# Two layers of linear attention and gated MLP on one core: GpSimd in the plan as exclusive with VectorE, GpSimd takes some rows, key weight first, new leads

## The chip, the cores and the metric

The kernel runs on 1 core of one Trainium2 chip. A core has five engines, each with its own instruction stream: TensorE (PE in the profile, with PEld for its weight loads), VectorE (DVE), ScalarE (ACT), GpSimd (POOL) and SyncE (SP, which only issues transfers here). The metric is device time in microseconds (us) for one execution. The kernel before takes 412.57 us, the median of 3 runs (409.76 to 413.67).

## The reference

The input is x, 2048 rows of 512 in bf16. Two layers, with the same weights in both, each do `x = x + A(layernorm(x))` and `x = x + B(layernorm(x))`:

```
def A(x):                                   # 32 heads of 16
    q, k, v = split(x @ wqkv)
    pq, pk = q @ w_phi, k @ w_phi           # per head, 16 x 16
    phi_q = concat(softmax(pq), softmax(-pq))
    phi_k = concat(softmax(pk), softmax(-pk))
    kv, z = phi_k.T @ v, phi_k.sum(rows)    # over all 2048 rows
    return ((phi_q @ kv) / (phi_q @ z + 1e-6)) @ wo
def B(x):                                   # F = 1376
    gate, up = x @ W_gate, x @ W_up
    return (relu(gate) * up) @ W_down
```

The sums kv and z run over all rows, so in each layer no row's attention can end before every row's keys are done.

## The kernel before

**Tiling.** The 16 tiles of 128 rows are worked in five slabs of 2, 4, 4, 4 and 2 tiles. All of x stays in SBUF (`x_sb`), as do the weights. For a slab, the names of stages are a letter code, the layer and the slab: `la` (layernorm before attention), `k` (keys and values), `q` (queries), `z` and `at` (denominators), `sp` (spreading the denominators over the features and scaling), `nm` (numerators), `wo` (output projection), `lg` (layernorm before the MLP), `gl` (gate and up), `d` (down projection); `fk` and `fq` fold w_phi into the key and query weights once.

**Layernorm** (`layernorm`, L720 on): VectorE takes statistics (L730, L731), ScalarE takes logarithm and exponential for the inverse deviation (L733, L735), and the row is normalized ("apply") on ScalarE (L747, for which VectorE first makes `nmr`, L739) or on VectorE (L750). TensorE then transposes the tile: four tiles at a time in 32 by 32 tiles of its array (L775), or one tile by four whole transposes (L612); ScalarE or VectorE copies the result into `yT` (L690, L693).

**Keys** (`keys`, L786 on): per tile, keys and values are multiplied (L799, L801, whose instructions carry the helper's line L608), two exponentials run on ScalarE (L803), VectorE sums them per head (`Zk`, L805) and takes the reciprocal (`rZk`, L807), the value is copied to `vsb`, and two products `vhat` of `vsb` and `rZk` (both in SBUF, 544 elements per partition) run on GpSimd, or on VectorE where a table says so (L815). TensorE adds exp(k) times vhat up in 128 x 32 tiles (L827) and VectorE adds the slab's sum to `kvsum` (L843). `sums` (L845) then spreads it into the block matrices `ZD` and `kvbd`.

**Attention** (`attend`, L874 on): `zz` and `zd` on TensorE, `Zs` on ScalarE, `zm`, `zden` on VectorE, logarithm and exponential on ScalarE (`zr`), `aT` on VectorE (L902). For slabs 0 and 1 a matmul spreads aT over the features (L973) and VectorE scales the exponentials `expq` by it (L988, L991). For slabs 2 to 4 aT goes out to DRAM and comes back spread (L912, L916), and `scale` multiplies four parts of expq by `abT` on VectorE (L958). Then the numerators (L928), their copies `oT`, and the output projection.

**Start.** TensorE runs eight warm-up matmuls. The key weight `Wknat` is transposed with w_phi's block matrix `BD` folded in: 16 transposes, four copies (`ftk0` to `ftk3`), 16 small matmuls, four casts into `Wkp` (`fck0` to `fck3`). SP issues x tile 0, x tile 1, the value weight wv, x tiles 2 to 7 and so on; ScalarE's queue issues w_phi and then the key weight in two halves.

**What sets the order.** Nothing is ordered by hand. `Program.op` collects operations with a planned occupancy and latency each. `schedule` lists them in order of a simulated clock: at each step it takes, over all engines, the ready operation with the smallest (start minus bonus, priority), and priority is the operation's number minus its stage's entry in the table `LEAD`; `BONUS` is a table too. `ENG` says per piece of work which engine does it. `plan` then puts semaphore waits where data depends on another engine. So the clock only fixes each engine's order; on the chip an engine runs its list and waits for semaphores.

An operation may be marked `port=True`. The plan then starts it no earlier than the end of the last GpSimd operation, and keeps GpSimd free until it ends:

```
if o.port and ported > s:
    s = ported
...
if o.port:
    free["pool"] = max(free["pool"], s + o.occ)
if o.eng == "pool" and not o.is_dma:
    ported = s + o.lat
```

Before, the mark stands at the apply on VectorE (L750) and at the scalings of expq with both inputs in SBUF (L958, L988). No semaphore comes of it.

Of the kernel before, what the change touches and what calls it, by code (L numbers as in the profile page):

```python
# [20 lines left out]
LEAD = {'': 1581,  # L21
 'at00': -9,
 'at01': -1074,
 'at02': -507,
 'at03': -757,
 'at10': -335,
 'at11': 762,
 'at12': -656,
 'at13': 331,
 'at14': -567,  # L30
 'd00': -5820,
 'd01': -1699,
 'd02': -13878,
 'd03': -2622,
 'd04': 3155,
 'd10': -13359,
 'd11': -2460,
 'd12': -1931,
 'd13': 71,
 'd14': -310,  # L40
 'fk': -480,
 'gl00': -2522,
 'gl01': 1205,
 'gl02': -5857,
 'gl03': -1218,
 'gl04': 504,
 'gl10': -2926,
 'gl11': -481,
 'gl12': -7344,
 'gl13': -46,  # L50
 'gl14': -166,
 'k00': 4572,
 'k01': 869,
 'k02': 459,
 'k03': -281,
 'k04': -136,
 'k10': 388,
 'k11': -124,
 'k12': -1352,
 'k13': 414,  # L60
 'k14': -1,
 'la00': -523,
 'la01': -375,
 'la02': 9240,
 'la03': 2125,
 'la04': -103,
 'la10': -743,
 'la11': -3565,
 'la12': -1372,
 'la14': 7230,  # L70
 'lg00': 199,
 'lg01': -221,
 'lg02': 153,
 'lg04': -687,
 'lg11': -282,
 'lg12': -264,
 'lg13': 794,
 'lg14': 2775,
 'nm00': 842,
 'nm01': 32,  # L80
 'nm02': 3263,
 'nm03': -579,
 'nm04': 406,
 'nm10': -741,
 'nm12': 16,
 'nm13': -1558,
 'nm14': -3291,
 'q00': 5078,
 'q01': -515,
 'q02': -692,  # L90
 'q03': 3551,
 'q04': -1249,
 'q10': -241,
 'q11': -69,
 'q12': -281,
 'q13': -2355,
 'q14': -138,
 'sp00': 803,
 'sp01': 206,
 'sp02': 643,  # L100
 'sp03': 36,
 'sp04': 2026,
 'sp10': 11,
 'sp11': -275,
 'sp12': -193,
 'sp13': -604,
 'sp14': 1242,
 'su0': -202,
 'su1': -6,
 'wo00': -564,  # L110
 'wo01': -1486,
 'wo02': -805,
 'wo03': -998,
 'wo04': 84,
 'wo10': 477,
 'wo11': 1154,
 'wo12': -216,
 'wo13': -222,
 'wo14': -8,
 'z00': -275,  # L120
 'z01': -232,
 'z02': -28,
 'z03': -803,
 'z04': 287,
 'z10': -247,
 'z11': 1911,
 'z12': 85,
 'z13': -5,
 'z14': 170}
BONUS = {'': 400,  # L130
 'at00': 1500,
 'at01': 400,
 'at02': 200,
 'at03': 200,
 'at04': 200,
 'at10': 400,
 'd03': 200,
 'd11': 800,
 'd12': 200,
 'fk': 400,  # L140
 'fq': 200,
 'gl03': 200,
 'gl04': 200,
 'gl11': 200,
 'gl12': 1500,
 'k12': 200,
 'la00': 400,
 'la01': 200,
 'la13': 200,
 'lg10': 400,  # L150
 'nm00': 200,
 'nm04': 200,
 'q11': 200,
 'sp00': 200,
 'sp01': 200,
 'sp03': 200,
 'sp10': 400,
 'sp11': 200,
 'sp13': 200,
 'su0': 800,  # L160
 'su1': 1500,
 'wo04': 400,
 'wo10': 400,
 'wo13': 200,
 'wo14': 200,
 'z03': 200,
 'z04': 200,
 'z10': 200,
 'z12': 400,
 'z13': 200}  # L170
HOLD = {}
ENG = {'ap/a00/0': 'act',
 'ap/a01/0': 'dve',
 'ap/a01/1': 'dve',
 'ap/a01/3': 'dve',
 'ap/a02/0': 'dve',
 'ap/a02/3': 'dve',
 'ap/a03/0': 'dve',
 'ap/a10/1': 'act',
 'ap/a11/1': 'act',  # L180
 'ap/a12/1': 'act',
 'ap/a12/2': 'act',
 'ap/a13/0': 'act',
 'ap/a13/3': 'act',
 'ap/a14/1': 'act',
 'ap/g01/0': 'act',
 'ap/g01/1': 'act',
 'ap/g01/3': 'act',
 'ap/g02/0': 'act',
 'ap/g02/3': 'act',  # L190
 'ap/g11/0': 'act',
 'ap/g12/2': 'act',
 'ap/g13/0': 'act',
 'ap/g13/2': 'act',
 'ap/g13/3': 'act',
 'ap/g14/1': 'act',
 'em/01/00': 'act',
 'em/01/01': 'dve',
 'em/01/02': 'act',
 'em/11/02': 'act',  # L200
 'em/11/03': 'dve',
 'fck3': 'act',
 'ftk0': 'dve',
 'ftq2': 'dve',
 'ftq3': 'dve',
# [3 lines left out]
 'ot/01/2': 'dve',  # L209
 'ot/01/3': 'dve',  # L210
 'ot/02/1': 'dve',
 'ot/02/2': 'dve',
 'ot/02/3': 'dve',
 'ot/03/3': 'dve',
 'ot/04/1': 'dve',
 'ot/04/2': 'dve',
 'ot/04/3': 'dve',
 'ot/10/2': 'dve',
 'ot/11/1': 'dve',
 'ot/13/0': 'dve',  # L220
 'ot/14/0': 'dve',
 'ot/14/1': 'dve',
 'ot/14/2': 'dve',
 'vc/0/5': 'dve',
 'vc/0/6': 'dve',
 'vc/1/0': 'dve',
 'vc/1/12': 'dve',
# [4 lines left out]
 'vc/1/8': 'dve',  # L232
 'vc/1/9': 'dve',
 'vh/0/10/1': 'dve',
 'vh/0/13/1': 'dve',
 'vh/0/15/0': 'dve',
 'vh/0/15/1': 'dve',
 'vh/0/7/0': 'dve',
 'vh/0/9/0': 'dve',
 'vh/1/0/1': 'dve',  # L240
 'vh/1/1/0': 'dve',
 'vh/1/10/0': 'dve',
 'vh/1/14/1': 'dve',
 'vh/1/15/0': 'dve',
 'vh/1/15/1': 'dve',
 'vh/1/3/1': 'dve',
 'vh/1/4/1': 'dve',
 'vh/1/5/0': 'dve',
 'vh/1/8/1': 'dve',
 'yc/a01/01': 'act',  # L250
 'yc/a01/03': 'act',
 'yc/a02/00': 'act',
 'yc/a02/03': 'act',
 'yc/a03/00': 'act',
 'yc/a03/02': 'act',
# [3 lines left out]
 'yc/a10/02': 'dve',  # L259
 'yc/a11/03': 'act',  # L260
 'yc/a12/01': 'act',
 'yc/a12/03': 'act',
 'yc/a13/00': 'dve',
 'yc/g00/1': 'dve',
 'yc/g01/00': 'dve',
 'yc/g01/01': 'act',
 'yc/g01/03': 'act',
 'yc/g02/00': 'dve',
 'yc/g04/00': 'dve',
 'yc/g04/02': 'dve',  # L270
 'yc/g04/03': 'act',
 'yc/g10/0': 'dve',
 'yc/g10/1': 'dve',
 'yc/g11/02': 'dve',
 'yc/g11/03': 'act',
 'yc/g12/01': 'act',
 'yc/g13/02': 'dve',
 'yc/g14/02': 'dve',
 'yc/g14/03': 'act'}
# [29 lines left out]
class Op:  # L309
    __slots__ = ("idx", "eng", "fn", "reads", "writes", "occ", "lat", "name", "is_dma", "nbytes",  # L310
                 "deps", "odeps", "users", "missing", "ready", "start", "finish", "cnt", "stream", "prio", "bonus", "port")

    def __init__(self, idx, eng, fn, reads, writes, occ, lat, name, is_dma=False, nbytes=0):
        self.idx, self.eng, self.fn = idx, eng, fn
        self.reads, self.writes = list(reads), list(writes)
        self.occ, self.lat, self.name = float(occ), float(lat), name
        self.is_dma, self.nbytes = is_dma, nbytes
        self.deps, self.odeps, self.users = set(), set(), []
        self.missing, self.ready = 0, 0.0
        self.start = self.finish = self.cnt = self.stream = None  # L320
        self.prio = idx
        self.bonus, self.port = 0.0, False


class Program:
# [4 lines left out]
    DMA_BW = 270.0  # L330

# [4 lines left out]
    def op(self, eng, fn, reads=(), writes=(), occ=100.0, lat=None, name="", bonus=0.0, port=False):  # L336
        o = Op(len(self.ops), eng, fn, reads, writes, occ, occ + 100.0 if lat is None else lat, name)
        o.bonus, o.port = bonus + BONUS.get(self.tag, 0.0), port
# [54 lines left out]
    def schedule(self):  # L393
        self.derive()
        free = {e: 0.0 for e in ENGINES}
        qfree = ported = 0.0
        ready = {e: [] for e in ENGINES}
# [9 lines left out]
        while left:  # L407
# [25 lines left out]
            for b in new_banks(o):  # L433
# [4 lines left out]
                if old is not None:  # L438
                    for x in old.ops:
                        if x.eng != "pe":  # L440
                            o.deps.add(x.idx)
            o.start = s
            if o.port:
# [83 lines left out]
def build_kernel(nc, A_x, A_wqkv, A_w_phi, A_wo, W_gate, W_up, W_down, out):  # L527
# [8 lines left out]
    with ExitStack() as ctx:  # L536
# [96 lines left out]

        load_x(0, 1)
        load_x(1, 2)
        dma("act", lambda e: e.dma_start(wphi[:], A_w_phi.rearrange("(kc hl) d f -> (hl d) kc f", hl=8)),
            writes=[R("wphi")], nbytes=131072, name="ld wphi")
        for c in (0, 2):
            dma("act", (lambda c: lambda e: e.dma_start(Wknat[:, c:c + 2, :], wqkv_v[:, c:c + 2, 512:1024]))(c),
                writes=R_Wnat["k"][c:c + 2], nbytes=262144, name="ld wk")  # L640
# [18 lines left out]
        op("dve", lambda e: e.memset(ones, 1.0), writes=[R("ones")] + [R("yT", NYT - 1, i) for i in range(4)], occ=480, name="ones")  # L659
# [5 lines left out]
        for i in range(NWARM):  # L665
            op("pe", lambda e: e.matmul(full(warm), ones[:, 0:128], ones[:, 0:512], start=True, stop=True),
               reads=[R("ones"), R("yT", NYT - 1, 0)], writes=[warm], occ=427, lat=640, name="warm")
        op("pool", lambda e: e.affine_select(ident[:], ones[:, 0:128], [[1, 128]], ALU.is_equal, 0.0, base=0, channel_multiplier=-1),
           reads=[R("ones"), R("yT", NYT - 1, 0)], writes=[R("ident")], occ=260, name="ident")
        op("pool", lambda e: e.affine_select(mask8a[:], ones[:, 0:8], [[-16, 8]], ALU.is_ge, 0.0, base=0, channel_multiplier=1),  # L670
           reads=[R("ones"), R("yT", NYT - 1, 0)], writes=[R("mask8a")], occ=150, name="mask8a")
# [48 lines left out]
        def layernorm(key, st, steps):  # L720
# [4 lines left out]
            for gi, step in enumerate(steps):  # L725
# [12 lines left out]
                if "act" in engs:  # L738
                    op("dve", (lambda t0, step: lambda e: e.scalar_tensor_tensor(nmr[:, t0:t0 + step, :], mv[:, t0:t0 + step, 0:1], -1.0, rstd[:, t0:t0 + step, :], ALU.mult, ALU.mult))(t0, step),  # L739
                       reads=Rmv + Ry, writes=[R("nmr", t) for t in ts], occ=75, lat=165, name="nmr")  # L740
                ybs = []
                for t, eng in zip(ts, engs):
# [6 lines left out]
                    else:  # L749
                        op("dve", (lambda t, yb: lambda e: e.tensor_scalar(ytile[:, yb, :], x_sb[:, t, :], mv[:, t, 0:1], rstd[:, t, :], op0=ALU.subtract, op1=ALU.mult))(t, yb),  # L750
# [385 lines left out]
```

## Time and profile before

| | |
|---|---|
| time, median of 3 runs | 412.57 us (409.76 to 413.67) |
| profiled execution | 414.23 us |
| its span, first to last instruction | 412.5 us |
| mean granted TensorE clock | 0.992 |
| TensorE busy | 396.0 us, 96% of the span |
| VectorE, ScalarE, GpSimd busy | 293.2, 209.5, 56.2 us |

An engine is busy while it has an instruction in flight; matmuls are pipelined, so their durations overlap, and "busy" is the union. A row of the timeline gives the start from the span's beginning, the length, the engine, the line of the kernel, the operation, what it writes and reads, its shape and the number of merged instructions; in brackets, how long the engine was idle before and who ended that. Instructions of helpers carry the helper's line: L608 is every plain matmul, L612 every whole transpose, L690 and L693 every copy on VectorE and ScalarE.

### The profile page before, as it was taken

The page shows a single profiled execution, that of the slowest core. Times are in us where ns is not written, and L with a number is a line of the kernel's source. Part 1 is how long each engine was busy: PE and PEld are TensorE (multiplying, and loading weights), DVE is VectorE, ACT ScalarE, POOL GpSimd, SP SyncE. Part 2 cuts the span into 40 slices and gives each one's busy share as a digit, 9 for nine tenths or more (in the row PEclk, how much of TensorE's full clock was granted, in tenths as well). Part 3 has the DMA queues.
Part 4 walks back from the last instruction along what each step waited for, and adds up shares of the span by engine and source line. Part 5 has one row for each costly group of instructions (what it writes and reads, how often), then busy time and mean ns, then how long its engine had stood idle before and what let it go on. Part 6 is the DMA issues. An engine that isn't in the chain of part 4 may idle for free.

```text
span 412.5 us, 11244 instructions
## 1 busy us (share of the span) xinstructions
PE 396.0 (96%) x4879; PEld 208.4 (51%) x4879; DVE 293.2 (71%) x586; ACT 209.5 (51%) x434; POOL 56.2 (14%) x55
## 2 busy tenths in 40 slices
PE   6899997999999998999999999999999999999997
PEld 3544543564444444445445745557444444444475
DVE  4899998897367779793988489638996354762253
ACT  4998998455304772247421477987335213432220
POOL 0068670000000232000600027000000000000000
PEclk9999998999999999999999999999999999999999
DMA  8960000300000003000100000011320000010011
GB/s 269 338 217 3 3 2 5 108 4 0 2 0 2 2 5 107 2 2 5 52 2 2 2 2 3 9 53 56 112 66 13 27 27 1 13 40 2 0 35 43
DMA packets 17922, 16.83 MB, mean 41 GB/s; under 512 B 3056, under 2 KB 16848, under 8 KB 17872
## 3 DMA queue, kind: packets, MB, share of 16 engines
q1 hardware_dynamic: 16656, 15.50, 11.6%
q8 instruction: 38, 0.62, 0.6%
q10 hardware_dynamic: 1216, 0.61, 0.5%
q14 instruction: 12, 0.10, 0.1%
HBM read 13.68 MB, written 2.42 MB: 39 GB/s over the span
## 4 chain that ended last, share of the span: by engine, by line
PE 79%; DVE 13%; ACT 3%; DMA 2%; issue 1%; POOL 1%; ACTq 0%; DVEq 0%
PE pb L608 72%; DVE Zk L805 3%; PE pb L886 2%; DVE vhat L815 2%; PE pb L775 2%; PE pb L827 2%; DMA hT<-in_A_wqkv_dram 1%; DVE stats L730 1%; DVE rZk L807 1%; PE pb L928 1%; DMA abT<-spread 1%; ACT expk L803 1%; PE pb L612 1%; DVE expq L991 1%; DVE vsb L690 1%
## 5 line engine op out<-in xcount | busy, mean ns | idle before, releaser
L1018 ACT ACTIVATE gate_sb<-pb 128x512 bf16<-128x512 f32 (+2 forms) x90 | 52.8, 587 | 113.0 <-PE pb L608 112.9
L1020 DVE TENSOR_TENSOR hT<-gate_sb,pb 128x512 bf16<-128x512 bf16 (+2 forms) x90 | 59.7, 670 | 64.5 <-PE pb L608 62.9
L608 PE MATMUL pb<-yT,Wu 128*128 128x512 bf16 (+3 forms) x440 | 94.6, 337 | 0.0
L608 PE MATMUL pb<-yT,Wg 128*128 128x512 bf16 (+3 forms) x440 | 92.6, 337 | 0.0
L815 POOL TENSOR_TENSOR vhat<-vsb,rZk 128x544 bf16<-128x544 bf16 x48 | 55.3, 1177 | 197.8 <-DVE rZk L807 116.6
L608 PE MATMUL pb<-Wd,hT 128*128 128x512 bf16 (+2 forms) x363 | 81.2, 373 | 0.0
L608 PEld LDWEIGHTS pb<-yT,Wg 128*128 128x128 bf16 (+1 forms) x440 | 43.2, 100 | 32.9 <-issue 0.7
L608 PEld LDWEIGHTS pb<-yT,Wu 128*128 128x128 bf16 (+1 forms) x440 | 43.1, 100 | 31.8 <-issue 0.6
L995 DVE TENSOR_TENSOR x_sb<-x_sb,pb 128x512 bf16<-128x512 bf16 x59 | 39.2, 680 | 22.8 <-PE pb L608 22.6
L608 PEld LDWEIGHTS pb<-Wd,hT 128*128 128x128 bf16 (+1 forms) x363 | 34.8, 98 | 39.4 <-issue 0.8
L803 ACT ACTIVATE expk<-pb 128x512 bf16<-128x512 f32 x64 | 35.4, 621 | 10.2 <-PE pb L608 8.8
L730 DVE BATCH_NORM_STATS2 stats<-x_sb 128x6 f32<-128x512 bf16 x60 | 39.4, 675 | 0.9 <-DMA x_sb<-in_A_x_dram 0.5
L805 DVE TENSOR_REDUCE Zk<-expk 128x64 f32<-128x1024 bf16 x32 | 37.6, 1189 | 1.7 <-ACT expk L803 1.6
L871 ACT ACTIVATE expq<-pb 128x512 bf16<-128x512 f32 x64 | 33.5, 623 | 6.1 <-PE pb L608 6.1
L608 PE MATMUL pb<-wv,yT 128*128 128x512 bf16 x128 | 34.5, 382 | 0.3 <-ACT expk L803 0.3
L608 PE MATMUL pb<-Wkp,yT 128*128 128x512 bf16 x128 | 34.1, 380 | 0.0
L608 PE MATMUL pb<-wo_sb,oT 128*128 128x512 bf16 x128 | 31.7, 392 | 0.8 <-ACT oT L693 0.8
L608 PE MATMUL pb<-yT,Wqp 128*128 128x512 bf16 (+1 forms) x160 | 31.6, 337 | 0.4 <-DVE yT L690 0.3
L693 ACT ACTIVATE yT<-pb 128x512 bf16<-128x512 bf16 (+1 forms) x36 | 19.5, 593 | 15.4 <-PE pb L775 14.4
L733 ACT ACTIVATE lnv<-mv,eps 128x4 f32<-128x4 f32 (+2 forms) x25 | 7.7, 307 | 34.7 <-DVE mv L731 34.2
L747 ACT ACTIVATE ytile<-x_sb,nmr,rstd 128x512 bf16<-128x512 bf16 x27 | 20.9, 815 | 1.4 <-DVE nmr L739 1.3
L608 PEld LDWEIGHTS pb<-wo_sb,oT 128*128 128x128 bf16 x128 | 12.2, 100 | 16.0 <-DVE oT L690 1.7
(77 smaller groups left out, 328.9 us busy)
## 6 DMA issues: line engine op xcount, KB each, us to landing
abT<-spread SPq DMA_DIRECT2D x32, 128.0 KB
out_dram<-x_sb SPq DMA_DIRECT2D x15, 128.0 KB, 4.0
x_sb<-in_A_x_dram SPq DMA_DIRECT2D x3, 512.0 KB
Wg<-in_B_W_gate_dram SPq DMA_DIRECT2D x1, 1376.0 KB
Wu<-in_B_W_up_dram SPq DMA_DIRECT2D x1, 1376.0 KB
Wd<-in_B_W_down_dram SPq DMA_DIRECT2D x1, 1280.0 KB
abT<-spread SPq DMA_DIRECT2D x16, 64.0 KB
hT<-in_A_wqkv_dram ACTq DMA_DIRECT2D x2, 256.0 KB
```

Source lines behind the costliest of these rows:

```text
L608: op("pe", lambda e: e.matmul(view(ps), lhsT, rhs, start=start, stop=stop), reads=reads, writes=[ps], occ=max(25.0, 0.4167 * n + 2.6), lat ...
L693: op("act", lambda e: e.activation(dst(), src(), ACT.Copy), reads=[ps] + reads, writes=writes, occ=115 + 0.714 * n, lat=240 + 0.714 * n, n ...
L730: op("dve", (lambda t, src: lambda e: e.bn_stats(stats[:, t, :], src()))(t, src), reads=[R("x", t) if ps is None else ps], writes=[R("st", ...
L747: op("act", (lambda t, yb: lambda e: e.activation(ytile[:, yb, :], x_sb[:, t, :], ACT.Identity, bias=nmr[:, t, :], scale=rstd[:, t, :]))(t ...
L775: ins = e.transpose(pss[i].b16()[:, n0:n0 + 32], ytile[r, yb, c * 128:(c + 1) * 128], ident[r, r], tile_position=(32 * i, 0))
L803: op("act", (lambda i, s, pk: lambda e: e.activation(expk[:, i, s, :], full(pk), ACT.Exp, scale=1.0 - 2.0 * s))(i, s, pk), reads=[pk], wri ...
L805: op("dve", (lambda i, zb: lambda e: e.tensor_reduce(Zk[:, zb, :], expk[:, i, :, :].rearrange("p s (h f) -> p (s h) f", f=16), AX.X, ALU.a ...
L815: op(eng, (lambda i, s, vb, rz: lambda e: e.tensor_tensor(vhat[:, i, s, :, :], vsb[:, vb, :, :], rZk[:, rz, s * 32:(s + 1) * 32].unsqueeze ...
L871: op("act", (lambda c0, s, ps: lambda e: e.activation(eqv(st)[:, c0:c0 + per, s, :], ps.f32()[:, 0:per * n].rearrange("p (c n) -> p c n", ...
L995: op("dve", lambda e: e.tensor_tensor(x_sb[:, t, :], x_sb[:, t, :], full(ps), ALU.add), reads=[R("x", t), ps], writes=[R("x", t)], occ=597 ...
L1018: op("act", (lambda m, gb, pg, k: lambda e: e.activation(gate_sb[0:m, gb, 0:k], pg.f32()[0:m, 0:k], ACT.Relu))(m, gb, pg, k), reads=[pg], ...
L1020: op("dve", (lambda m, gb, hb, pu, k: lambda e: e.tensor_tensor(hT[0:m, hb, 0:k], gate_sb[0:m, gb, 0:k], pu.f32()[0:m, 0:k], ALU.mult))(m, ...
```

## The change

1. More VectorE operations with both inputs in SBUF are marked exclusive in the plan: `nmr`, `vhat` where VectorE does it, the two `zdw` and `kvbd` of `sums`, `zden` and `aT`.
2. An apply may run on GpSimd, planned at 640 ns: 19 do (8 in layer 0 and 7 in layer 1 ahead of attention, 1 and 3 ahead of the MLP). ScalarE's go from 27 to 13 and VectorE's from 37 to 32.
3. A scaling of expq (`scale`) may run on GpSimd: 11 of 24 do (six of 1024 elements, five of 512).
4. GpSimd's vhat go from 48 to 45, VectorE's from 16 to 19. Copies change engines too: the fold copies ftk1 and ftk3 by the table, and ftk0 by its missing entry, are on ScalarE as ftk2 was.
5. At the start ScalarE issues the first half of the key weight ahead of w_phi, and SP the second half ahead of x tile 1.
6. The plan knows four tilings of TensorE's array (`mode`) and adds 95 ns where it changes; the planned costs of tiled groups are lowered in turn.
7. The tables LEAD and BONUS are new throughout.
8. The `ones` of the start, which lie in the last buffer of yT, now carry that buffer's names in full, so that its first use waits for them.

```
-LEAD = {'': 1581, ...
+LEAD = {'': 82, ...
- 'q00': 5078,
- 'q01': -515,
+ 'q00': -57,
+ 'q01': -5419,
...
+ENG = {'ap/a00/0': 'pool',
+ 'ap/a00/1': 'pool',
+ 'ap/a01/0': 'pool',
+ 'ap/a01/1': 'pool',
+ 'ap/a01/2': 'pool',
...
+ 'es/02/0': 'pool',
+ 'es/02/1': 'pool',
...
- 'ftk0': 'dve',
+ 'fcq3': 'dve',
+ 'ftk1': 'act',
+ 'ftk3': 'act',
...
+    SWITCH = 95.0
...
+            if o.eng == "pe" and o.mode != mode:
+                s = max(s, free["pe"] + self.SWITCH)
             o.start = s
+            if o.eng == "pe":
+                mode = o.mode
...
+        def load_wk(eng, c):
+            dma(eng, lambda e: e.dma_start(Wknat[:, c:c + 2, :], wqkv_v[:, c:c + 2, 512:1024]), writes=R_Wnat["k"][c:c + 2], nbytes=262144, name="ld wk")
+
         load_x(0, 1)
-        load_x(1, 2)
+        load_wk("act", 0)
+        load_wk("sp", 2)
         dma("act", lambda e: e.dma_start(wphi[:], A_w_phi.rearrange("(kc hl) d f -> (hl d) kc f", hl=8)),
             writes=[R("wphi")], nbytes=131072, name="ld wphi")
-        for c in (0, 2):
-            dma("act", (lambda c: lambda e: e.dma_start(Wknat[:, c:c + 2, :], wqkv_v[:, c:c + 2, 512:1024]))(c),
-                writes=R_Wnat["k"][c:c + 2], nbytes=262144, name="ld wk")
+        load_x(1, 2)
...
-                        op("dve", (lambda t, yb: lambda e: e.tensor_scalar(ytile[:, yb, :], ...
-                           ..., occ=322, lat=405, name=f"apply{t}", port=True)
+                        op(eng, (lambda t, yb: lambda e: e.tensor_scalar(ytile[:, yb, :], ...
+                           ..., occ=322 if eng == "dve" else 640, lat=405 if eng == "dve" else 710, name=f"apply{t}", port=eng == "dve")
...
-                       ..., name=f"vh{t}")
+                       ..., name=f"vh{t}", port=eng == "dve")
...
-        def scale(st, c):
+        def scale(L, st, c):
...
+            eng = ENG.get(f"es/{L}{st}/{c}", "dve")
+            t = 64 + 1.06 * n if eng == "dve" else 100 + 3.6 * n
+            op(eng, lambda e: e.tensor_tensor(part, part, abT[:, c]..., ALU.mult),
+               ..., occ=t, lat=t + 91, name=f"em{st}", port=eng == "dve")
...
-            op("dve", ... Zs ... zr ..., occ=64 + 2.08 * w, lat=155 + 2.08 * w, name="aT")
+            op("dve", ... Zs ... zr ..., occ=64 + 2.08 * w, lat=155 + 2.08 * w, name="aT", port=True)
```

## The prediction

> **What bounds the kernel now.** I read the page's first part, then busy time by stretch, then the waits, then single instructions in the timeline, and last the shortest and longest of a kind. First the page, busy time of each engine:
>
> ```profile
> PE 396.0 (96%) x4879; PEld 208.4 (51%) x4879; DVE 293.2 (71%) x586; ACT 209.5 (51%) x434; POOL 56.2 (14%) x55
> ```
>
> TensorE is busy for all but 16.5 us of the 412.5. The change alters neither the matmuls nor their sizes, so a gain can only come out of TensorE's idle time, its stretches at half clock, and its changes of tiling. Where these lie, by stretch (start:end, length, then busy us of PE, PEld, DVE, ACT and POOL, granted clock, DMA share, GB/s):
>
> ```profile
> 5.00:8.30 3.30, 0.90 (x15) 0.72 (x15) 0.23 (x3) 1.09 (x3) 0.00 (x0) 0.99 1.06 359
> 8.30:11.70 3.40, 3.40 (x32) 3.12 (x30) 2.57 (x6) 2.46 (x5) 0.00 (x0) 0.50 1.10 354
> ...
> 20.00:60.00 40.00, 39.12 (x795) 19.82 (x797) 39.93 (x68) 37.88 (x80) 28.91 (x26) 1.00 0.19 64
> 60.00:70.00 10.00, 6.47 (x312) 3.87 (x301) 7.82 (x23) 7.88 (x22) 0.00 (x0) 0.98 0.01 3
> 70.00:75.00 5.00, 4.33 (x42) 1.32 (x40) 3.65 (x9) 3.42 (x8) 0.00 (x0) 0.69 0.07 16
> ...
> 140.00:165.00 25.00, 23.53 (x350) 11.12 (x349) 21.34 (x31) 13.59 (x28) 7.11 (x6) 1.00 0.14 46
> ...
> 240.00:300.00 60.00, 58.60 (x1024) 33.59 (x1023) 46.99 (x97) 43.55 (x99) 10.18 (x8) 1.00 0.14 43
> ```
>
> Four places. At 5.0 to 8.3 TensorE is idle for 2.4 us; at 8.3 to 11.7 it has half the clock. From 20 to 60 (the keys of layer 0) VectorE is full (39.93 of 40) and ScalarE nearly so; TensorE looks busy only because query matmuls fill its gaps. At 60 to 75 the sums are ready, that filler has largely been used up, and TensorE idles 3.53 + 0.67 = 4.2 us and runs part of it at half clock (0.69 of 5.00: 1.55 us lost). At 140 to 165 and 240 to 300 it idles 1.47 and 1.40. From 300 on it is solid up to the tail, so nothing is to be had there.
>
> Who ends the wait at 5 us (waits, stretch 4 to 9), and what follows it (timeline: start, length):
>
> ```profile
> PE pb L612 <- DMA hT<-in_A_wqkv_dram: 2.4, 1, 2.4
> ```
>
> ```profile
> 7.98 0.81 PE L612 MATMUL pb<-ident,hT 128*128 128x128 bf16 x8 [2.40 <-DMA hT<-in_A_wqkv_dram]
> 8.30 1.09 DVE L690 COPY hT<-pb 128x512 bf16<-128x512 bf16 x3 [3.03 <-PE pb L612]
> ...
> 8.62 0.60 ACT L693 ACTIVATE hT<-pb 128x512 bf16<-128x512 bf16 x1 [2.26 <-PE pb L612]
> ```
>
> The second half of the key weight lands at 7.98; four copies follow, three on VectorE and one on ScalarE side by side, and then the fold's products.
>
> VectorE against GpSimd, timeline of each:
>
> ```profile
> 151.42 1.32 DVE L902 TENSOR_TENSOR aT<-Zs,zr 128x256 bf16<-128x256 f32 x1
> ...
> 153.24 0.72 DVE L815 TENSOR_TENSOR vhat<-vsb,rZk 128x544 bf16<-128x544 bf16 x1
> ```
>
> ```profile
> 150.30 2.16 POOL L815 TENSOR_TENSOR vhat<-vsb,rZk 128x544 bf16<-128x544 bf16 x2 [8.68 <-DVE rZk L807]
> 153.28 1.64 POOL L815 TENSOR_TENSOR vhat<-vsb,rZk 128x544 bf16<-128x544 bf16 x1 [0.82 <-DVE rZk L807]
> ```
>
> The aT that starts inside GpSimd's pair ends just after that pair (152.74 against 152.46); the GpSimd one that starts inside a VectorE vhat is longer by 0.54. Whoever is second waits. By tile (ns: minimum/median/maximum):
>
> ```profile
> L815 POOL TENSOR_TENSOR vhat<-vsb,rZk x48: 1098/1103/1662, 23.6 to 253.8; 128x544 bf16<-128x544 bf16 x48
> L815 DVE TENSOR_TENSOR vhat<-vsb,rZk x16: 709/1144/1666, 40.5 to 254.3; 128x544 bf16<-128x544 bf16 x16
> ```
>
> ```profile
> L958 DVE TENSOR_TENSOR expq<-expq,abT x24: 405/678/864, 80.1 to 306.4; 128x1024 bf16<-128x1024 bf16 x16, 128x512 bf16<-128x512 bf16 x8
> L988 DVE TENSOR_TENSOR expq<-expq,abT x13: 416/417/419, 67.4 to 284.7; 128x512 bf16<-128x512 bf16 x13
> ```
>
> The vhat on VectorE are not marked as exclusive in the plan, and their median is 1.6 times their minimum. The scalings of expq are marked already: 36 of those 37 keep their bare time. So the mark, though it sets no semaphore, does hold on the chip.
>
> **The change part by part**, each against the profiled execution (414.23; span 412.5; 1.7 around it; the median of the three shown is 412.57, so what I work out is taken off the median).
>
> (1) Key weight first, on two queues. ScalarE issues its half before wphi, and SP issues the other after x tile 0 only; x tile 1 and wv go behind 256 KB more. Ahead of the second half lie now 128 + 512 + 16 KB; the first 5 us moved 174 GB/s x 5 = 0.87 MB. So it should be there at about 5 us, when the warm-up matmuls end (5.04). Worth the idle 2.4; between 0 and that. wv and x tile 1 come 256 KB / 359 GB/s = 0.7 us later: wv is first used at 11.15, x tile 1 at 4.35 ahead of VectorE's idle 3.03, which hides it. wphi is needed at 3.67 by a 0.68 VectorE product that has until the fold's products: the same idle hides it.
>
> (2) The four fold copies all go to ScalarE. Before, they end 9.39 - 7.98 = 1.4 after the landing. Four at 0.54 (a pair on ScalarE takes 1.08) behind 0.32 of transposes end 2.5 after it: +1.1 on the path. (1) and (2): -1.3. Half clock at 8.3 to 11.7: 3.40 busy at half, so 0 to -1.7; TensorE still waits for copies there, so I take -0.5, nearer to 0.
>
> (3) The key stretch. Applies of layer 0 go from 9 ScalarE, 7 VectorE to 4, 4 and 8 on GpSimd. VectorE: three applies fewer at 0.404 = -1.2; three fold copies at 0.416 = -1.25; seven vhat at 0.71 = 5.0 for six that take 6.6 now = -1.7; one nmr of 0.92 back to 0.15 = -0.8; two more value casts at 0.67 and one Wqp cast at 0.69 = +2.0. Together -2.9. ScalarE: five applies at 0.815, two value copies at 0.631, one Wqp copy at 0.62, less three fold copies at 0.596: -4.2. TensorE itself does no less: what it gains is that fewer query matmuls are used as filler before 60 and more are left for 60 to 75 (the leads say so too: q01 from -515 to -5419). There 4.2 idle + 1.55 clock = 5.75 is the ceiling, 0 the floor; I take -3.0, about VectorE's 2.9.
>
> (4) Collisions at 140 to 300. TensorE waits for vhat of either engine 2.3 us in all (tile view, PE's row). Bare vhat would free most: 0 to -2.3; I take -1.5.
>
> (5) GpSimd's new work: 19 applies of 512 elements, whose duration no row shows: at least VectorE's 0.404, at most GpSimd's vhat at 1.10. I take 0.9, nearer to GpSimd's own row, as it is the same engine. Eleven scalings of expq: by elements of the vhat row 1.10 x 1024/544 = 2.07 for six and 1.04 for five, against 0.68 and 0.42 on VectorE. Two big ones in a slab end 4.1 after their transfers where four on VectorE take 2.7: 1.4 late, covered by GLU matmuls (75 to 140 has TensorE busy for 64.9 of 65). Layer 1's applies, three in a row on GpSimd (slabs 1 and 3) 2.7 for 1.2, have the same cover; with it gone they would cost 1.5 each. Taken: +0.5, of 0 to +3.
>
> The Trainium skill, GPSIMD Engine Reference, section 3.1, speaks against this part: it advises VectorE for elementwise work, as GpSimd takes about twice as long there, and it puts GpSimd's tightest loop at 769 ns for 512 elements. No run here shows such an operation on GpSimd yet. By that estimate the eight applies of rival C take 6.2 us, and C would not come about by them alone.
>
> (6) New collisions: GpSimd reads SBUF 75 times instead of 48. Of the 37 marked scalings one collided, for 0.45. A plan that drifts may bring five times that on VectorE, a quarter of it on the path: +0.5, of 0 to +3.
>
> (7) Leads, bonuses, costs of tiled groups. In the starts of single matmuls a 512-column one follows its like after 216 ns, a tiled group's first follows after about 310: 94 ns a change, some 130 changes. Grouping may save 30 of them, or waste as many: -3 to +3, and I take -0.5, close to nothing.
>
> Sum: -1.3 - 0.5 - 3.0 - 1.5 + 0.5 + 0.5 - 0.5 = -5.8. That is 408.4 for a profiled execution and 406.8 for the median.
>
> **Rivals.** A, more: the half clock goes at both places and 60 to 75 is filled: -2.4 + 1.1 - 1.7 - 5.75 - 2.3 - 0.5 = -11.5, 401. For it: VectorE and ScalarE both get time back. Against: the chain of waits crosses 62 to 75 through zm, aT, expq and oT, work of VectorE and ScalarE that no filler shortens.
>
> B, nothing: the keys stay bound by VectorE, the fold's copies eat the earlier weight, and the filler is spent as before. Only (4) and a little of (1) stay: -1.5, 411.
>
> C, slower: GpSimd becomes the bound of the key stretch. It has 25 vhat at 1.10 less overlaps (28.9 for 26 now), and eight applies in order between them. From its first vhat at 23.6 to 59.6 it has 36.0 - 28.9 = 7.1 us free. Eight applies at 1.10 take 8.8: late by 1.7, and if each holds a VectorE operation for half its time, 4.4 more: +6.1, 418.6. It decides once the applies and their waits pass 7.1, 0.9 each. For it: VectorE is full. Against: some applies (a00, a01) come before the first vhat. The Trainium skill, SBUF — State Buffer, section on who interferes with whom, says that the loser of the shared port blocks fully and that the order of issue decides; the aT row (1.32 for 0.42) agrees.
>
> **How the numbers follow.** Forecast 0.42, A 0.18, B 0.24, C 0.16. About 1% (4.1 us) is what a measurement of this kernel can tell from no change. Forecast and A are faster: 0.60; B is the same: 0.24; C slower: 0.16. Predicted 406.8. The range leaves out half of A and most of C: 400.0 to 416.0; the forecast's own is 403 to 410.
>
> **What would show it.** (1) the first fold transposes' wait is gone and its copies stand in a row on ScalarE; (3) TensorE's idle time at 57 to 75 under 2 us; (4) VectorE's vhat at a median near 0.71, aT never 1.3; (5) a GpSimd apply at 0.8 to 1.0. I am wrong if VectorE's vhat or aT still take over 1 us, if kv products wait for GpSimd, or if the bubble behind the sums stays at 4 us.

## The result: 428.0 us, 3.9% slower, and the profile after

The changed kernel takes 428.02 us (median of 4 runs, 426.84 to 431.36) against 413.12 for the kernel before in the same set of runs: ratio 1.039, 95% interval 1.030 to 1.047. Forecast were 406.8 and a range up to 416. The profiled execution has a span of 425.9 us for 412.5. (In the experiments, too, the ratio is to the kernel before in the same set of runs, where its median was 412.3 to 413.4. The ratios compare all runs of both kernels, so they can differ by some tenths of a per cent from the ratio of the two medians.)

Line numbers have moved by 62 to 66 (L608 is now L670, L750 is L814, L815 is L879). First the busy time, from the page of the changed kernel:

```profile
PE 391.2 (92%) x4823; PEld 209.7 (49%) x4879; DVE 285.3 (67%) x564; ACT 200.9 (47%) x419; POOL 109.5 (26%) x82
```

VectorE and ScalarE have 8 to 9 us less to do, as was meant. GpSimd has 53 us more, and TensorE's idle time has gone from 16.5 to some 25 to 35 us. (That cannot be read closer: 56 of the 4879 matmul records are missing here, none before, and each leaves a hole that looks like an idle 0.1 to 0.3 us. The rows "PE pb L670 <- issue" below, with many short waits, are such holes, so I go by waits that name a releaser.) By stretch, columns as in the prediction:

```profile
5.00:8.30 3.30, 2.26 (x33) 2.09 (x31) 1.81 (x4) 2.00 (x4) 2.08 (x1) 1.00 0.99 329
8.30:11.70 3.40, 1.92 (x17) 0.96 (x16) 2.85 (x7) 2.11 (x7) 2.07 (x1) 1.00 1.10 354
11.70:20.00 8.30, 4.81 (x43) 2.72 (x42) 5.44 (x13) 6.39 (x14) 4.74 (x3) 0.97 1.08 324
20.00:60.00 40.00, 34.69 (x647) 18.40 (x656) 35.36 (x62) 30.28 (x64) 31.49 (x26) 0.92 0.20 69
```

From 20 to 60 VectorE is no longer full (35.36 for 39.93) and neither is ScalarE (30.28 for 37.88), yet the stretch is longer. Nobody is the bound by its own work; they wait. TensorE's waits of the changed kernel, longest first (total, times, longest):

```profile
PE pb L839 <- POOL ytile L814: 10.4, 4, 4.6
PE pb L674 <- POOL ytile L814: 4.3, 4, 1.4
PE pb L670 <- issue: 4.2, 24, 0.3
PE pb L950 <- issue: 1.7, 1, 1.7
```

No wait of TensorE for `ytile` stands in this view of the kernel before. The transposes (L839, L674) wait 14.7 us for rows that GpSimd normalizes. (The single wait of 1.7 us is taken up in the last section.) How one wait comes about, GpSimd's and then TensorE's timeline:

```profile
15.26 6.19 POOL L814 TENSOR_SCALAR ytile<-x_sb,mv,rstd 128x512 bf16<-128x512 bf16 x3 [4.12 <-DVE hT L754]
```

```profile
21.59 0.69 PE L839 MATMUL pb<-ident,ytile 32*128 32x32 bf16 x64 [4.60 <-POOL ytile L814]
```

Three applies in a row take 6.19 us: 2.07 each, where the plan has 0.64. The transposes of the slab can start only behind the third, the keys behind the transposes, and so on down the line. The same again at the end of layer 0, for slab 3 of layer 1:

```profile
239.66 6.19 POOL L814 TENSOR_SCALAR ytile<-x_sb,mv,rstd 128x512 bf16<-128x512 bf16 x3 [19.16 <-DVE hT L1086]
```

```profile
245.99 0.65 PE L839 MATMUL pb<-ident,ytile 32*128 32x32 bf16 x64 [2.96 <-POOL ytile L814]
```

Where the 13.4 us of the span arise is seen from the moment when the sums over all rows are ready in each layer. Tile view of `ZD`, which is written right behind the sums; the two times are its first and last write, in layer 0 and in layer 1, of before and of after:

```profile
L849 DVE TENSOR_TENSOR ZD<-kvsum,mask x4: 183/188/192, 62.2 to 257.4; 128x32 bf16<-128x32 f32 x4
```

```profile
L913 DVE TENSOR_TENSOR ZD<-kvsum,mask x4: 185/190/192, 69.4 to 271.6; 128x32 bf16<-128x32 f32 x4
```

7.2 us are lost ahead of layer 0's sums and 14.2 by layer 1's; at the end it is 13.4, so behind layer 1's sums nothing more is lost.

The marks, on the other hand, do what they say (minimum/median/maximum, ns; after):

```profile
L879 DVE TENSOR_TENSOR vhat<-vsb,rZk x19: 660/716/853, 52.4 to 268.7; 128x544 bf16<-128x544 bf16 x19
```

```profile
L966 DVE TENSOR_TENSOR aT<-Zs,zr x10: 284/417/426, 73.6 to 297.5; 128x256 bf16<-128x256 f32 x6, 128x128 bf16<-128x128 f32 x4
```

VectorE's vhat had a median of 1.144 us and go at 0.716; aT had a worst case of 1.32 and now 0.43.

### The profile page after: what moved, and what is told of

The parts are those of the page before. It is cut to its first block, busy times and chain, and to the rows that moved or that the text cites. A ratio compares the mean times of both kernels' runs of the same rounds, so it can differ in the third digit from the quotient of the medians.

```text
span 425.9 us, 11195 instructions
## 1 busy us (share of the span) xinstructions
PE 391.2 (92%) x4823; PEld 209.7 (49%) x4879; DVE 285.3 (67%) x564; ACT 200.9 (47%) x419; POOL 109.5 (26%) x82
## 4 chain that ended last, share of the span: by engine, by line
PE 73%; DVE 11%; POOL 8%; issue 3%; ACT 2%; DMA 2%; SPq 0%; POOLq 0%; DVEq 0%
PE pb L670 65%; POOL ytile L814 7%; DVE x_sb L1061 2%; DVE stats L794 2%; PE pb L950 2%; PE pb L839 2%; PE pb L891 2%; DVE Zk L869 2%; POOL vhat L879 1%; PE pb L992 1%; PE pb L674 1%; DMA abT<-spread 1%; DVE vsb L754 1%; DMA x_sb<-in_A_x_dram 1%; DMA spread<-aT 0%
## 5 line engine op out<-in xcount | busy, mean ns | idle before, releaser
L670 PE MATMUL pb<-yT,Wg 128*128 128x512 bf16 (+3 forms) x435 | 92.7, 336 | 1.0 <-issue 0.8
L670 PE MATMUL pb<-yT,Wu 128*128 128x512 bf16 (+3 forms) x432 | 91.3, 336 | 0.4 <-issue 0.2
L670 PE MATMUL pb<-Wd,hT 128*128 128x512 bf16 (+2 forms) x347 | 80.0, 372 | 1.5 <-issue 1.0
L814 POOL TENSOR_SCALAR ytile<-x_sb,mv,rstd 128x512 bf16<-128x512 bf16 x19 | 39.6, 2091 | 147.2 <-ACT rstd L799 65.6
L879 POOL TENSOR_TENSOR vhat<-vsb,rZk 128x544 bf16<-128x544 bf16 x45 | 50.7, 1152 | 37.6 <-DVE rZk L871 30.9
L670 PEld LDWEIGHTS pb<-yT,Wu 128*128 128x128 bf16 (+1 forms) x440 | 43.7, 100 | 32.2
L670 PEld LDWEIGHTS pb<-yT,Wg 128*128 128x128 bf16 (+1 forms) x440 | 43.1, 100 | 32.8 <-DVE yT L754 0.4
L670 PEld LDWEIGHTS pb<-Wd,hT 128*128 128x128 bf16 (+1 forms) x363 | 34.6, 98 | 38.8 <-issue 1.2
L670 PE MATMUL pb<-wv,yT 128*128 128x512 bf16 x125 | 34.9, 387 | 0.5 <-issue 0.3
L670 PE MATMUL pb<-Wkp,yT 128*128 128x512 bf16 x119 | 33.5, 385 | 1.1 <-issue 0.7
L670 PE MATMUL pb<-yT,Wqp 128*128 128x512 bf16 (+1 forms) x151 | 32.4, 350 | 1.1 <-issue 1.0
L1024 POOL TENSOR_TENSOR expq<-expq,abT 128x1024 bf16<-128x1024 bf16 (+1 forms) x11 | 18.5, 1684 | 54.0 <-DMA abT<-spread 34.7
L670 PE MATMUL pb<-wo_sb,oT 128*128 128x512 bf16 x122 | 29.8, 385 | 1.4 <-ACT oT L757 0.8
L757 ACT ACTIVATE yT<-pb 128x512 bf16<-128x512 bf16 (+1 forms) x34 | 17.6, 561 | 27.8 <-PE pb L839 25.9
L754 DVE COPY yT<-pb 128x512 bf16<-128x512 bf16 (+1 forms) x36 | 13.0, 395 | 14.3 <-PE pb L839 12.4
```

The lines of the kernel that those rows point to most:

```text
L670: op("pe", lambda e: e.matmul(view(ps), lhsT, rhs, start=start, stop=stop), reads=reads, writes=[ps], occ=max(25.0, 0.4167 * n + 2.6), lat ...
L757: op("act", lambda e: e.activation(dst(), src(), ACT.Copy), reads=[ps] + reads, writes=writes, occ=115 + 0.714 * n, lat=240 + 0.714 * n, n ...
L814: op(eng, (lambda t, yb: lambda e: e.tensor_scalar(ytile[:, yb, :], x_sb[:, t, :], mv[:, t, 0:1], rstd[:, t, :], op0=ALU.subtract, op1=ALU ...
L879: op(eng, (lambda i, s, vb, rz: lambda e: e.tensor_tensor(vhat[:, i, s, :, :], vsb[:, vb, :, :], rZk[:, rz, s * 32:(s + 1) * 32].unsqueeze ...
L1024: op(eng, lambda e: e.tensor_tensor(part, part, abT[:, c].rearrange("p (s n) -> p s n", s=2)[:, :, 0:n], ALU.mult), reads=Re + [R("abT", c ...
```

## The experiments

Theory 1 was that the applies on GpSimd carry the loss, since each takes 2.07 us. The rivals: the scalings of expq on GpSimd (2), and the new order of the work, whoever does it (3). The difficulty is that any change of engine or cost makes the planner order everything anew. So most of these kernels keep the planned order: the schedule is made as before, and only then are operations moved to another engine's list, at the place that their planned start gives them.

### 1. The applies to VectorE, order kept (e1_apply_dve)

```diff
         prog.schedule()
+        for o in prog.ops:
+            if o.eng == "pool" and o.name.startswith("apply"):
+                o.eng = "dve"
```

> The changed kernel with its planned order of every engine kept, only the 19 applies that GpSimd does are put into VectorE's list, at the place that their planned start gives them. Theory 1 (an apply takes 2.07 to 2.08 us on GpSimd, planned 0.64, and TensorE waits 14.7 us for it in the profile of the changed kernel): nearly all of the loss of 15 us goes, 411 to 416 us, and no wait of TensorE for an apply above 1 us in all. Rival 2 (the 11 scalings on GpSimd carry the loss): 426 to 429. Rival 3 (the new order of the work, whatever engine does it): 422 to 429.

Measured: 413.93 us, ratio to before 1.002 (0.999 to 1.006). The whole loss goes with these 19 instructions. (TensorE's waits for applies, now VectorE's, come to 1.4 + 0.4 us; under 1 was expected.) Theory 1 stands; rivals 2 and 3 fall as main causes, since the scalings on GpSimd and the new order are all in this kernel. The tile view of `ZD` says the same: the sums are ready at 63.6 in layer 0, not at 69.4, and ZD's last write in layer 1 is at 258.0, not at 271.6.

```profile
L913 DVE TENSOR_TENSOR ZD<-kvsum,mask x4: 184/188/192, 63.6 to 258.0; 128x32 bf16<-128x32 f32 x4
```

One more rival can be settled from the profiles: that GpSimd's applies cost by holding up VectorE. VectorE's busy time, in which a held-up instruction counts at its full length, is 285.3 us in the changed kernel and 284.0 in experiment 8, which has the same instructions on VectorE and short ones in place of the 19 applies. So such collisions are worth 1.3 us of VectorE's time, not 15.

### 2. The scalings to VectorE, order kept (e2_scale_dve)

The same edit, with operations named `em` in place of `apply`.

> The changed kernel with its planned order kept, only the 11 scalings of expq go from GpSimd's list to VectorE's. Theory 1 (the applies): 425 to 430, no change beyond the noise. Rival 2 (the scalings, 18.5 us of GpSimd): 415 to 420. Rival 3 (order): 425 to 430.

Measured: 429.79 us, ratio 1.043 (1.037 to 1.049): nothing comes back, so the scalings cost nothing where they stand. Their length was predicted well, 2.07 us for 1024 elements; the tile view of the changed kernel has 2.12 as the median, which is one of the six of that size:

```profile
L1024 POOL TENSOR_TENSOR expq<-expq,abT x11: 1154/2120/2126, 91.0 to 314.1; 128x1024 bf16<-128x1024 bf16 x6, 128x512 bf16<-128x512 bf16 x5
```

That the MLP's matmuls cover them, as step 5 had it, fits, and was not tested apart.

### 3. The same 19 applies to GpSimd in the kernel before, order kept (e3_before_pool)

```diff
         prog.schedule()
+        for o in prog.ops:
+            if o.name.startswith("apply") and o.name.split("/", 1)[1] in ON_POOL:
+                o.eng = "pool"
```

> The kernel before with its planned order kept, only the same 19 applies are moved to GpSimd's list, from VectorE's or ScalarE's. Theory 1: the loss comes back in the old order, 422 to 432, with TensorE waiting for applies of 2.07 us in the order of 10 us. Rival 2 (scalings) and rival 3 (new order): 412 to 416, as neither is in this kernel.

Measured: 421.57 us, ratio 1.022 (1.016 to 1.028). More than half of the loss comes in the old order too: 8 to 9 us instead of 15, a little under the 422 to 432 that were expected. TensorE's named waits for GpSimd's applies come to 6.7 us, where some 10 were expected. In the tile view of `ZD` the sums of layer 0 are as late as in the changed kernel, 69.6, but between the two layers nothing more is lost (264.4 for 257.4 before):

```profile
L850 DVE TENSOR_TENSOR ZD<-kvsum,mask x4: 184/188/191, 69.6 to 264.4; 128x32 bf16<-128x32 f32 x4
```

So the applies are the cause, and the order sets how much of them shows.

### 4. A lighter apply (e5_one_op) and the forms of it (e8_forms)

The edit of e5, with the call shortened:

```diff
-   e.tensor_scalar(y, x, mean, rstd, op0=ALU.subtract, op1=ALU.mult)
+   e.tensor_scalar(y, x, rstd, None, op0=ALU.mult)                    # GpSimd's only
```

> The changed kernel, but GpSimd's apply only multiplies by the inverse deviation: the subtraction of the mean is left out of those 19 rows' tiles. If GpSimd's time goes by the number of operations in the instruction, an apply takes about 1.1 us, as the vhat product of 544 elements does (1.10), and with theory 1 about half of the loss goes: 418 to 423. If it goes by elements alone it stays at 2.07 us and the time at 426 to 430. Rival 2 and rival 3: 425 to 430 whatever the apply takes.

> The changed kernel as a measurement of GpSimd alone: of the 19 applies on GpSimd those of tiles 0, 4, 8, 12 stay as they are; tiles 1, 5, 9, 13 use two operations with constants instead of the row's mean and deviation; tiles 2, 6, 10, 14 one operation with a constant; tiles 3, 7, 11, 15 only copy the row. So the rows of those tiles are not normalized. With pointers 2.07 us for two operations and 1.56 for one were measured. If the row pointers cost nothing, two constants take 2.07 and one takes 1.56; if the pointers are what is dear, two constants take 1.0 to 1.2. A copy: 0.5 to 1.05.

Measured: 420.37 us for one operation (ratio 1.019, 1.013 to 1.024), and 421.56 for the mixed forms (a single run). Neither expectation of the duration was right: the instruction with one operation takes 1.56 us, not 1.1 and not 2.07. That the time lies within 418 to 423 is luck, since that range was worked out for 1.1 us. The tile view of e5:

```profile
L815 POOL TENSOR_SCALAR ytile<-x_sb,rstd x19: 1557/1562/2089, 5.3 to 340.5; 128x512 bf16<-128x512 bf16 x19
```

The four forms, tile view of the mixed kernel:

```profile
L817 POOL COPY ytile<-x_sb x7: 608/612/936, 16.3 to 325.7; 128x512 bf16<-128x512 bf16 x7
L814 POOL TENSOR_SCALAR ytile<-x_sb,mv,rstd x6: 2075/2082/2087, 4.8 to 237.4; 128x512 bf16<-128x512 bf16 x6
L816 POOL TENSOR_SCALAR ytile<-x_sb x4: 1497/1500/1609, 14.8 to 341.8; 128x512 bf16<-128x512 bf16 x4
L815 POOL TENSOR_SCALAR ytile<-x_sb x2: 1924/1924/1924, 8.8 to 139.1; 128x512 bf16<-128x512 bf16 x2
```

For 512 elements: a copy 0.61, one operation with a constant 1.50, two with constants 1.92, two with the row's values 2.08. The pointers to row values cost 0.06 to 0.16, a second operation about 0.4 to 0.5; most of the price is there as soon as it is an arithmetic operation with a scalar and no longer a copy (0.61 to 1.50). So the copy lies in its expected range, and the constants near the case of cheap pointers. The plan's 0.64 is about what a copy takes.

### 5. Which of the 19 (e10_singles_stay, e11_start_dve)

The edit of experiment 1, for the stages a00, a01, g00, a11, a13 (12 applies), and for a00 and a01 alone (5).

> The changed kernel with its planned order kept; the 12 applies of the stages where two or three stand in a row on GpSimd or where the transposes follow at once (a00, a01, g00, a11, a13) go into VectorE's list, the 7 that stand alone among other engines' applies (a02, a03, a04, a12, g11, g12, g13) stay on GpSimd at 2.07 us. If the place decides and not the number: 412 to 417, the loss gone with 12 of 19. If every apply costs alike (15 us over 19): 418 to 420.

> The changed kernel with its planned order kept; only the five applies of the start (a00 and a01) go into VectorE's list. In the profile of the changed kernel TensorE waits 1.0, 1.4 and 4.6 us for these, and runs at half clock from 19.5 to 26.3 after them. If these waits reach the end: 428 less 7 us, less up to 3 of the clock, 418 to 421. If the key stretch gives it back as it did with the earlier weight: 423 to 427.

Measured: 414.53 us for the first (ratio 1.005, 1.002 to 1.008): seven applies of 2.07 us stay on GpSimd, one to a stage, and cost 0.2 to 0.8% against the kernel before, and next to nothing against the 413.93 of experiment 1. In the tile view of that kernel:

```profile
L814 POOL TENSOR_SCALAR ytile<-x_sb,mv,rstd x7: 2074/2076/2373, 21.5 to 335.6; 128x512 bf16<-128x512 bf16 x7
```

So the other 12 carry the loss: those that stand two or three in a row, and those with the transposes right behind them. Which of these two traits counts for more was not tested.

The second takes 422.89 us (1.024, 1.019 to 1.029), between the two ranges that were expected. The five applies of the start are worth 5.1 us by the medians, and about 6 by the two ratios (1.039 and 1.024). TensorE's waits for them sum to 7.0 in the changed kernel. Without them the sums of layer 0 come 6.4 us earlier (63.0 for 69.4), the last ZD of layer 1 6.9 earlier (264.7 for 271.6) and the end of the profiled execution 6.3 (419.6 for 425.9), so nearly all of these waits reaches the end:

```profile
L913 DVE TENSOR_TENSOR ZD<-kvsum,mask x4: 185/188/193, 63.0 to 264.7; 128x32 bf16<-128x32 f32 x4
```

### 6. The plan told the truth (e4_true_cost)

The part of the line that changes:

```diff
-   occ=322 if eng == "dve" else 640, lat=405 if eng == "dve" else 710
+   occ=322 if eng == "dve" else 2050, lat=405 if eng == "dve" else 2150
```

> The changed kernel with one number of the plan changed: an apply on GpSimd is planned at 2050 ns (latency 2150) instead of 640 (710), so the order of the work is made anew around it; the same 19 applies stay on GpSimd. Theory 1a (the loss is the plan's error: with the right cost the order puts other work under the applies): 412 to 418. Theory 1b (the applies themselves are too long where they stand, at the start and behind the sums, and no order hides them): 420 to 428.

Measured: 439.81 us, ratio 1.065 (1.061 to 1.070), slower than both expectations. The plan is made anew, and LEAD and BONUS were not. TensorE's longest waits for applies are now for ScalarE's and VectorE's (4.5 and 3.7 us). This does not tell 1a from 1b; it fits that the tables suit one plan only. The next two say the same.

### 7. The other parts by themselves (e6_before_loads, e7_before_marks, e9_loads_fixed)

e6: the kernel before with the new order of the first loads. e7: the kernel before with the new marks. Both are planned anew with the old tables. e9: the kernel before with its order kept and only the loads moved after the schedule was made.

> The kernel before with only the new order of the first loads (key weight first, on two queues), planned anew with the old tables. If the earlier weight is worth what the prediction said, TensorE's wait of 2.4 us for it goes and the time falls by 1.3 to 2.4 us: 410.5 to 412.5. If it is spent again behind the sums or by another order: 412.5 to 416.

> The kernel before with only the new marks of exclusive VectorE operations (nmr, vhat, zdw, kvbd, zden, aT), planned anew with the old tables. If the mark does what the prediction said, VectorE's vhat stand at a median near 0.71 us (1.14 before) and the time falls by 1 to 3 us: 410 to 412.5. If the collisions were off the path, the medians fall and the time stays: 412.5 to 415. If the old tables do not fit the new plan: over 415.

> The kernel before with every engine's order of work kept; only the first loads are issued in the new order (first half of the key weight ahead of w_phi on ScalarE's queue, second half on SP's between x tiles 0 and 1). If step 1 of the prediction holds, TensorE's wait of 2.4 us for the second half goes and the time falls by 1.4 to 2.4 us (here three of the four fold copies stay on VectorE, so nothing is given back): 410.7 to 411.7. Rival (the key stretch is bound by VectorE and takes the gain back): 412.5 to 414.

Measured: e6 417.94 us (1.012, 1.009 to 1.016), e7 447.04 (1.084, 1.079 to 1.088), e9 411.92 (0.998, 0.995 to 1.002). In e7 VectorE's vhat have a median of 0.719, and still it is the slowest kernel of all: the marks worked, and the order that they led to with the old tables cost 34 us. So e6, which lies above both of its ranges, and e7 do not price their edit. e9 does: the earlier weight is worth 0.4 us, not told from nothing, and between the two ranges that were expected. Its waits, VectorE's and then TensorE's timeline at the start:

```profile
5.47 0.69 DVE L681 TENSOR_TENSOR hT<-wphi,mask 128x512 bf16<-128x512 bf16 x1 [1.24 <-DMA wphi<-in_A_w_phi_dram]
...
7.01 1.08 DVE L690 COPY hT<-pb 128x512 bf16<-128x512 bf16 x3
```

```profile
8.13 0.40 PE L612 MATMUL pb<-ident,ytile 128*128 128x128 bf16 x4 [2.05 <-ACT ytile L747]
8.37 1.72 PE L608 MATMUL pb<-hT 128*128 128x128 bf16 x16
```

w_phi now lands behind the weight, and the product with it, the statistics of x tile 1 and nmr stand ahead of the copies in VectorE's list. The copies start 1.3 us earlier (7.01 for 8.30). TensorE's wait of 2.4 us for the weight is gone, but in its place TensorE waits 2.05 us for the first row that ScalarE normalizes, and the fold's products start only 0.65 us earlier (8.37 for 9.02). The sums of layer 0 come no earlier at all (62.3 for 62.2).

### 8. The changed kernel as its plan sees it (e12_copies)

GpSimd's applies only copy the row: 0.61 us, about the planned 0.64.

> The changed kernel with its planned order kept; the 19 applies on GpSimd only copy the row (those rows are not normalized), which took 0.61 us on GpSimd in the run of forms, about the 0.64 that the plan gives an apply. So this is the changed kernel as its plan sees it. If the prediction's sum is right but for the length of an apply: 405 to 409. If the rest of the change is worth nothing (as with the applies on VectorE): 411 to 414.

Measured: 411.00 us, ratio 0.996 (0.993 to 0.998). The sums of layer 0, from the tile view of `ZD`:

```profile
L914 DVE TENSOR_TENSOR ZD<-kvsum,mask x4: 183/190/193, 61.2 to 255.8; 128x32 bf16<-128x32 f32 x4
```

So with an apply as short as the plan assumes, the change would be worth 0.4%, not the 1.4% that I forecast: the time lies at the edge of "worth nothing" and short of 405 to 409. 428.0 - 411.0 = 17.0 us is the price of the 1.46 us by which each of the 19 applies is longer than such a copy (27.7 us in all), with the clock and the waits behind it.

No experiment pointed to a kernel that beats the one before by more than the noise: e9 is 0.4 us below it, inside its interval, and e12 leaves the normalization of 19 row tiles out.

## Why the prediction was wrong, point by point

**The step that failed is (5)**, GpSimd's new work. I bounded an apply "at most" by GpSimd's vhat at 1.10 and took 0.9; it takes 2.07. The vhat row was the only long GpSimd row in the trace, but it is another instruction, a product of two tensors, and I took the same engine for the same price per element. A bound has to be of the same operation, or be no bound.

The sum also has no term at all for the five applies of the start: step (3) books them as time that VectorE and ScalarE save, and nothing says that TensorE would wait for them, without a reason given. Without these five on GpSimd the kernel is 5 to 6 us shorter (e11). The one price that (5) has for applies in a row, 1.5 each in layer 1, it took as covered; TensorE waits 2.5 and 3.0 us there.

With 2.07 the sum of rival C would have pointed to slower, since its eight applies need 16.6 us where it has 7.1 free, but for a wrong reason: five of the eight run ahead of the first vhat (24.32 in the changed kernel), and the other three need 6.2. The section of the Trainium skill that I cited (GPSIMD Engine Reference, 3.1) gives 769 ns for 512 elements as the best case of a tight loop. A copy took less here, 0.61 us, and arithmetic with scalars 1.50 to 2.08, so that figure prices neither and the measurement decides. The apply's 2.07 is also five times VectorE's 0.404, where the prediction has "about twice".

**Rival C** had the right side and engine, and 0.16 of the chance. Its place was wrong. GpSimd is not the bound by the amount of its work (31.49 of 40 busy in the key stretch); it is the latency of a single apply right ahead of the transposes at 7 and at 11 us, and of three in a row ahead of those at 22, all at the start, where no MLP matmuls stand by to cover them. In layer 1, where I had seen cover ("the same cover" of MLP matmuls), TensorE waits 2.5 and 3.0 us from 143 and 243 on in spite of it. I even wrote what it costs with the cover gone (1.5 each), and then took +0.5 for all of step (5).

**(1)** TensorE's wait of 2.4 us for the weight is gone, in every kernel with the new loads. That w_phi is hidden was wrong (VectorE waits 1.65 for it in the changed kernel, 1.24 in e9), and in e9, where it stands alone, nothing of the 1.3 to 2.4 us reaches the sums.

**(2)** The fold copies end at 8.48 for 9.39: 0.9 earlier; forecast 1.3. The rest is the wait for the first apply on GpSimd, which stands ahead of the last four of the fold's transposes: in e1 and e12, without that wait, the copies end at 7.95 and 7.84, so up to there the term was about right. The half clock at 8.3 is gone, as hoped for at most; but in the changed kernel it comes back after the wait of 4.6 us (0.92 over the 40 us from 20 to 60).

**(3)** Failed too, apart from the applies. In e12, where they are short, the sums are ready at 61.2 for 62.2: 1.0 earlier, where VectorE's 2.9 and the start's 1.3 would make it 4.2. And "more query matmuls are left" was false: by the weight loads, whose records are complete, all 48 query matmuls of the first three slabs lie ahead of the sums in the changed kernel, 44 before, and none in the 20 us behind them, 4 before. The bubble that I took 3.0 off has grown. From 57 to 75 TensorE idles 6.75 us in e12 and 4.28 before, and the granted clock is 0.81 for 0.91 (columns as in the prediction, before and e12):

```profile
57.00:75.00 18.00, 13.72 (x442) 6.72 (x440) 14.40 (x32) 14.30 (x34) 2.58 (x3) 0.91 0.03 7
57.00:75.00 18.00, 11.25 (x428) 6.39 (x428) 12.03 (x30) 9.72 (x24) 0.00 (x0) 0.81 0.01 4
```

2.25 of the 2.5 us of growth are the waits of (7). For the rest I take it that filler is worth nothing behind the sums as long as a chain through VectorE and ScalarE sets the length there; that fits the rows and was not tested. I had written it against rival A and not against my own -3.0.

**(4)** Right in the mechanism and small in the size. In e12 TensorE no longer waits for a vhat at all (2.3 us before), and its idle time at 140 to 165 is 0.52 us for 1.47, 0.95 of the 1.5. From 240 to 300 nothing is gained (1.94 for 1.40, some of it missing records).

**(6)** Collisions did come in the changed kernel: an apply on VectorE takes up to 1.27 us (0.41 before), nmr up to 0.95 in spite of its mark (0.92 before), and of the two additions of epsilon, which have one SBUF input and carry no mark, one takes 0.165 and the other, inside a scaling on GpSimd, 1.416. They make a few us of VectorE's time; how much of it delays the end was not measured, but one of the long applies (at 40.00) stands on the chain that ended last.

**(7)** I took 0.5 us off for better grouping of the tiled matmuls. In this order tiled groups stand closer around the sums, and there TensorE has waits that I did not expect (last section): two of 1.3 and 1.7 us in e12 on the chain around the sums, one of 0.78 before. From the sums to the first gate matmul it is 18.5 us in e12 (61.2 to 79.7) and 17.0 before. The wait of 1.7 lies in that stretch and is as long as what is lost there, so e12's earlier sums are spent by it.

## What to carry to other kernels

Before moving work to another engine, run that very instruction once there and look at its row; a row of the same engine with another operation can be off by a factor of two or three (0.61, 1.10, 1.50 and 2.07 us for 512 to 544 elements). An engine that is idle most of the time still has latency: give it single pieces that nobody waits for soon (the seven of e10 cost next to nothing), and not two or three in a row ahead of the engine that bounds the kernel. And where a planner's tables were searched for one set of costs, price an edit with the order frozen, since the tables may fit no other plan (e6 and e7, planned anew, were 1 and 8% slower than the kernel before).

## What the runs showed of the hardware that I had not expected

GpSimd's prices above. And waits of TensorE that look like waits for instructions. In the kernel with copies (e12), two pieces of work that are one operation in the program, without any wait inside, are cut in two, at the keys' product (L892) and at `zd` (L951), TensorE's timeline:

```profile
58.79 0.28 PE L892 MATMUL pb<-vhat,expk 128*32 128x34 bf16 x16
60.40 0.28 PE L892 MATMUL pb<-vhat,expk 128*32 128x34 bf16 x16 [1.33 <-issue]
...
61.92 0.64 PE L951 MATMUL pb<-expq,ZD 128*32 128x64 bf16 x47 [0.49 <-DVE ZD L914]
64.26 0.44 PE L951 MATMUL pb<-expq,ZD 128*32 128x128 bf16 x17 [1.70 <-issue]
```

A tiled group of 64 matmuls and 64 weight loads is through in about 0.6 us. The transfers of the instruction queue (page of before: "q8 instruction: 38, 0.62" MB, so 16 KB each) end at 58.93 and 62.86 in this kernel, and TensorE goes on 1.47 and 1.40 us later. In five kernels (before, after, e1, e10, e12) TensorE has ten waits of over 0.4 us for which the profile names no releaser, and all ten end 1.2 to 1.5 us after the end of one of these transfers. Nine stand around the sums of layer 0, where tiled groups follow each other with hardly a 512-column matmul between. The tenth (1.07 us, to 22.16 in e12) stands in a single tiled group behind 512-column matmuls, and most transfers bring no wait. All this fits TensorE running out of instructions; it was seen, and not tested by an experiment. The Trainium skill, Runtime: NRT & Kernel Launch, section Instruction fetch mechanics, states the blocks of 16 KiB and 256 instructions, and calls the cost of crossing one mostly hidden. The trace bears out the blocks (38 transfers of 16 KB for TensorE's 9758 matmuls and weight loads, 257 each). Most of the 38 crossings bring no wait; if these ten waits are crossings, the cost shows there, at 0.7 to 1.7 us.
